# Attention output products in another order: four whole-array products, then eight half-array products

## The chip, the core and the metric

The kernel runs on one core of a Trainium2 chip. Five engines work side by side on one on-chip memory: the matrix engine (TensorE, PE in the profile, its weight loads PEld), VectorE (DVE), ScalarE (ACT), GpSimd (POOL) and SyncE (SP), which here only issues DMA transfers. A matrix product takes a stationary operand that is loaded into the array and streams a moving operand through it; the result goes to PSUM, an accumulator memory in banks. The metric is the device time of one execution in microseconds (us); less is better.

## The reference, cut to what matters

```
# 4 batches, 8 heads, 768 tokens, 48 features per head, all float32
for t in range(S):
    state = alpha[:, :, t, :, None] * state + einsum('bhd,bhe->bhde', k[:, :, t], v[:, :, t])
    y[:, :, t] = einsum('bhd,bhde->bhe', q[:, :, t], state)
x = y.transpose(0, 2, 1, 3).reshape(3072, 384)
h = x @ w_in;  x = (max(h, 0) + m_alpha * min(h, 0)) @ w_out          # expert layer 1, d_ff 2048
h = x @ w_in2; out = where(h >= 1, h, where(h <= -1, 0, (h + 1)**2 / 4)) @ w_out2   # layer 2
```

The first part is a linear attention whose state decays by a factor per feature and step. The two expert layers that follow take nearly all of the arithmetic.

## The kernel before, in words

**Attention in chunks.** The 3072 tokens are cut into 24 chunks of 128, six to a batch. For one chunk, all eight heads together, four functions run in turn. `fetch` brings q, k and alpha to a layout with features on the partitions (tile `T`): up to chunk 9 by transpositions on the matrix engine (`at_in_pe`), from chunk 10 on by a transposition on VectorE (line 205, `X<-nat`) and 16 DMA transfers (line 211, `T<-X`). `at_alpha` builds the running products of the decays on VectorE, `at_qk` scales keys and queries (`K2`, `Q2`). `at_scores` multiplies them for each head (line 247, `sc`), masks the result into `A` (line 252) and, unless the chunk is the last of its batch, transposes `K2` (`kt`, `KT`). `at_out` makes the output `y` of the chunk.

**The output of a chunk.** Two heads form a pair p, so y has four column blocks of 128 tokens, all in one PSUM bank. Each block is the sum of a state product (line 271: the stationary operand is `bd[:, p, :]`, the block-diagonal state of both heads, 128 rows by 128 columns, so it takes the whole array) and two score-value products (line 274: one per head a, with 128 rows by 64 columns of values, so each takes half of the array's columns and writes 64 of the 128 partitions). In the first chunk of a batch there is no state, and the state products are left out. All operands are float32, and each such product runs as two passes on the matrix engine, each with its own weight load: a chunk has 8 passes of state products and 16 of score-value products. Unless the chunk is the last of its batch, eight small products `ds` (line 288) follow, from which VectorE renews `bd` (line 315); GpSimd then divides it by the next chunk's decays (line 332).

**What happens to y.** ScalarE copies y to the high part of `xs`, the input of layer 1 (line 300), VectorE the rest (line 305). The fourth column block holds the last sixteen features of six pairs' heads in a packed form; after the startup it goes by way of `x3` (lines 302 and 307) and six DMA transfers to its places (line 323).

**Startup and the main loop.** The first four chunks run before anything else (`startup`). There the packed block is not moved by DMA: the products of p = 3 come first, ScalarE copies the block to `y3` (line 280), and a further whole-array product per block p = 0 to 2 (line 295, stationary operand `sel`) adds it in. Then the expert layers run in steps: a block of 512 tokens has 16 steps, one per 128 columns of d_ff; in each a product group `hp` (line 429), the activation on VectorE, ScalarE and GpSimd (`g`, `gh`, `gl`; lines 444 to 453), and the second product one step later (line 462 in layer 1, 473 in layer 2). Six blocks are layer 1, six are layer 2. The remaining 20 chunks of attention are laid between the steps of layer 1 by `groups` and `run_slots`; a chunk takes four slots. During the first block the weights of layer 1 are also loaded, joined from 64-bit words (lines 360 to 368) and split. Every engine takes its instructions in the order in which the program is written; there is no scheduler. SyncE's queue carries all DMA issues, in that order too: per chunk 16 of line 211, then the three loads of the next chunk's q, k and alpha (line 157), weight loads (352 to 355), a store (398), the six of line 323 and a load of v (162).

Of the kernel before, what the change touches and what calls it, by code (L numbers as in the profile page):

```python
# [22 lines left out]
def kernel(  # L23
# [13 lines left out]
    nc = tc.nc  # L37
# [5 lines left out]
    NP = H // 2  # L43
    NFC = DFF // P
    ND = DM // P
# [20 lines left out]
    ps_o = main.enter_context(tc.tile_pool(name="ps_o", bufs=1, space=PSUM))  # L66
    ps_a = main.enter_context(tc.tile_pool(name="ps_a", bufs=3, space=PSUM))

# [1 line left out]
    ident = const.tile([P, P], F32, name="ident")  # L70
    mask = const.tile([P, C], F32, name="mask")
    zrev = const.tile([P, NP, SEG], BF16, name="zrev")
# [11 lines left out]
    bd = const.tile([P, NP, P], F32, name="bd")  # L84
# [8 lines left out]
    own = {}  # L93

    def spare_tile(key, shape, name):
        """A tile of the startup in the place of a weight tile that comes later."""
        if key not in own:
            own[key] = wpool.tile(shape, F32, tag=next(spare), name=name)
        return own[key]

    def shared_row(g):
        """Where the last two heads' sixteen features g stand in their own tile."""
        return 16 * g if g < 3 else 64 + 16 * (g - 3)

    sel = spare_tile("sel", [P, ND, P], "sel")

    def setup_consts():
# [31 lines left out]
            if c > 0:  # L139
                nc.gpsimd.memset(v_of(c)[:, :, D:64], 0.0)  # L140

# [1 line left out]
    st = {}  # L143

    NPE = 10
# [16 lines left out]
        eng.dma_start(out=v_of(c)[:, :, 0:D], in_=v[b, :, t0:t0 + C, :].rearrange("h t d -> t h d"))  # L162

    def flag(src, i, col):
        """Sums, into a column, how far the decays lie outside one end of the chunked form's range."""
        junk = p1.tile([P, 768], mybir.dt.uint8, tag="junk", name="junk")
        nc.scalar.activation(junk[:, 0:src.shape[1]], src, AF.Relu, scale=(-1.0, 1.0)[i],
                             bias=bias2[:, i:i + 1], accum_out=acc[:, col:col + 1])
# [6 lines left out]
    NFL = H * S * D // P // 768  # L175

    def load_flags(i):
        """The decays of the first batches, whose chunks pass without their flags."""
        t = p3.tile([P, 768], F32, tag="wst", name="al", padded_shape=[P, 4 * DM])
        nc.sync.dma_start(out=t, in_=alpha[i // NFL].rearrange("h t d -> (h t d)")  # L180
                          .rearrange("(p n) -> p n", p=P)[:, i % NFL * 768:(i % NFL + 1) * 768])
        own["al", i] = t
# [79 lines left out]
    def at_out(c, xdst, startup=False, mid=None):  # L262
        s = st[c]
        vc = v_of(c)
        pool, tag = (ps_h, "h") if startup else (ps_a, "at")
        first, last = c % CPB == 0, c % CPB == CPB - 1
        y = pool.tile([P, NP, C], F32, tag=tag, name="y")

        def emit_y(p, done=True):
            if not first:  # L270
                nc.tensor.matmul(out=y[:, p, :], lhsT=bd[:, p, :], rhs=s["Q2"][:, p, :],  # L271
                                 start=True, stop=False)
            for a in range(2):
                nc.tensor.matmul(out=y[64 * a:64 * a + 64, p, :], lhsT=vc[:, 2 * p + a, :],  # L274
                                 rhs=s["A"][a][:, p, :], start=first, stop=done)

        if startup:
            emit_y(ND)
            y3 = spare_tile(("y3", c % 2), [P, C], "y3")
            nc.scalar.copy(out=y3, in_=y[:, ND])  # L280
        else:
            for p in range(NP):
                emit_y(p)
        if not last:
            ds = pool.tile([P, NP, D], F32, tag=tag, name="ds", padded_shape=[P, NP, P])
            for h in range(H):
                lo = HALVES[h % 2][0]
                nc.tensor.matmul(out=ds[lo:lo + D, h // 2, :], lhsT=s["KT"][:, h // 2, lo:lo + D],
                                 rhs=vc[:, h, 0:D], start=True, stop=True)
        if mid:  # L290
            mid()
        if startup:
            for p in range(ND):
                emit_y(p, False)
                nc.tensor.matmul(out=y[:, p, :], lhsT=sel[:, p, :], rhs=y3, start=False, stop=True)
        xs, o = xdst
        hi, lo = xs[:, 0, :, o:o + C], xs[:, 1, :, o:o + C]
        if not startup:
            x3 = p1.tile([P, 2, C], F32R, tag="x3", name="x3")
        nc.scalar.copy(out=hi, in_=y[:, 0:ND])  # L300
        if not startup:
            nc.scalar.copy(out=x3[:, 0], in_=y[:, ND])

        def low():
            nc.vector.tensor_sub(out=lo, in0=y[:, 0:ND], in1=hi.bitcast(F32))  # L305
            if not startup:
                nc.vector.tensor_sub(out=x3[:, 1], in0=y[:, ND], in1=x3[:, 0].bitcast(F32))

        def state():
            for l, r in HALVES:  # L310
                nv = bd[l:r, :, l:r]
                if first:
                    nc.vector.tensor_copy(out=nv, in_=ds[l:r])
                elif not last:
                    nc.vector.tensor_add(out=nv, in0=ds[l:r], in1=nv)

        for f in (state, low) if startup else (low, state):
            f()
        st.pop(c)
        for g in range(0 if startup else 6):  # L320
            r = shared_row(g)
            d0 = 48 if g % 2 == 0 else 112
            nc.sync.dma_start(out=xs[d0:d0 + 16, :, g // 2, o:o + C].bitcast(F32),
                              in_=x3[r:r + 16].bitcast(F32))

    def at_decay(c):
        """The state before chunk c, divided by the chunk's decays: block diagonal, by pairs."""
        if c % CPB:
            R = st[c]["R"]
            for lo, hi in HALVES:  # L330
                nv = bd[lo:hi, :, lo:hi]
                nc.gpsimd.tensor_mul(out=nv, in0=nv, in1=R[lo:hi, :, 0:1].to_broadcast([D, NP, D]))

# [1 line left out]
    wt = {}  # L335
    stg = {}
    wide = w_in1.dtype != F32
# [18 lines left out]
        stg[layer, fc] = t  # L356

    def words_f32(lo, hi, t, nbias):
        """lo, hi: the words of the float64 t, scaled so that the exponent is rebased."""
        nc.scalar.activation(hi.bitcast(F32), t[:, :, 1].bitcast(F32), AF.Copy, scale=2.0 ** -112)  # L360
        nc.scalar.activation(lo, t[:, :, 0], AF.Relu, scale=2.0 ** -29, bias=nbias)

    def join_f32(f, lo, hi):
        """f: the float of the high word shifted by three, its sign, and the low word's top bits."""
        fu = f.bitcast(U32)
        nc.vector.scalar_tensor_tensor(out=fu, in0=hi, scalar=3, in1=lo,  # L366
                                       op0=ALU.logical_shift_left, op1=ALU.bitwise_or)
        nc.vector.scalar_tensor_tensor(out=fu, in0=hi, scalar=0x80000000, in1=fu,  # L368
                                       op0=ALU.bitwise_and, op1=ALU.bitwise_or)
# [49 lines left out]
    def w_out_of(layer, fc):  # L419
        return [w[:, DM:2 * DM] for w in wt[layer, fc]]  # L420

# [1 line left out]
    def emit_h(layer, fc, xs, n):  # L423
        wh, wl = w_in_of(layer, fc)
        hp = ps_h.tile([P, n], F32, tag="h", name="hp", padded_shape=[P, 512])
# [47 lines left out]
                    nc.tensor.matmul(out=ops[t], lhsT=g[:, t * P:(t + 1) * P], rhs=w,  # L473
                                     start=first, stop=last)

# [1 line left out]
    blk = []  # L477
    t0 = 0
    for n in BLOCKS1:
# [52 lines left out]
    done = [0]  # L532
# [7 lines left out]
    with tc.manual_schedule():  # L540
# [84 lines left out]
            nc.scalar.copy(out=xs[:, 0, d, :], in_=t)  # L625
            nc.vector.tensor_sub(out=xs[:, 1, d, :], in0=t, in1=xs[:, 0, d, :].bitcast(F32))

        # startup: the attention of the first block, chunks overlapped
        load_chunk(0, nc.sync)
        setup_consts()  # L630
        load_chunk(1, nc.sync)
# [67 lines left out]
                if 0 <= i - 4 < 2 * NFB * NFL:  # L699
                    flag(own["al", (i - 4) // 2], i % 2, i - 4)  # L700

# [1 line left out]
    tot = const.tile([P, 1], F32, name="tot")  # L703
    nc.vector.tensor_reduce(out=tot, in_=acc, op=ALU.add, axis=mybir.AxisListType.X)
    fps = ps_a.tile([P, 512], F32, tag="at", name="fps")
# [12 lines left out]


def general_attention(tc, q, k, v, alpha, xT_d):  # L720
    """The recurrence itself, a scan over time for each column of the state: any decay."""
    nc = tc.nc
    B, H, S, D = q.shape
    P = 128
# [1 line left out]
    with ExitStack() as es:  # L726
        cst = es.enter_context(tc.tile_pool(name="g_const", bufs=1))
        one = es.enter_context(tc.tile_pool(name="g_one", bufs=1))
        two = es.enter_context(tc.tile_pool(name="g_two", bufs=2))
# [16 lines left out]
        with tc.For_i(0, B * H, 1) as i:  # L746
            tr = []
            for n, src in enumerate((q, k, alpha, v)):
# [3 lines left out]
                t = one.tile([D, S], F32, tag=f"g_t{n}", name=f"g_t{n}")  # L752
# [6 lines left out]
            y = ps_y.tile([D, 1024], F32, tag="g_y", name="g_y")  # L759
            for e in range(D):  # L760
                vb = ps_v.tile([D, 1024], F32, tag="g_vb", name="g_vb")
                for t, n in spans:
                    nc.tensor.matmul(out=vb[:, t:t + n], lhsT=row[:, e, :], rhs=vT[:, t:t + n],
                                     start=True, stop=True)
                kv = two.tile([D, S], F32, tag="g_kv", name="g_kv")
                nc.vector.tensor_mul(out=kv, in0=vb[:, 0:S], in1=kT)
                state = two.tile([D, S], F32, tag="g_st", name="g_st")
# [4 lines left out]
                for t, n in spans:  # L772
                    nc.tensor.matmul(out=y[:, t:t + n], lhsT=col[:, e, :], rhs=pr[:, t:t + n],
                                     start=(e == 0), stop=(e == D - 1))
# [3 lines left out]


def general_layer(tc, layer, x_src, w_in, w_out, m_alpha, dst, B, to_f32):  # L780
    """One expert layer in float32 products, 128 tokens at a time."""
    nc = tc.nc
    P = 128
    DFF, DM = w_out.shape[0], x_src.shape[0] * P if layer else x_src.shape[1]
    NFC, ND = DFF // P, DM // P
    S = 768
    with ExitStack() as es:
        cst = es.enter_context(tc.tile_pool(name="g_w", bufs=1))
        two = es.enter_context(tc.tile_pool(name="g_l2", bufs=2))
# [11 lines left out]
        for fc in range(NFC):  # L801
            for w, src in ((wi, w_in[:, fc * wn * P:(fc + 1) * wn * P].rearrange("(a p) f -> p a f", p=P)),
# [5 lines left out]
                t = two.tile([P, wn * DM], U32, tag="g_ws", name="g_ws")  # L808
# [3 lines left out]
        with tc.For_i(0, B, 1) as b:  # L812
            for n in range(S // P):
# [9 lines left out]
                for fc in range(NFC):  # L823
                    hp = ps_h.tile([P, P], F32, tag="g_h", name="g_h")
                    for c in range(ND):
                        nc.tensor.matmul(out=hp, lhsT=wi[:, fc, c * P:(c + 1) * P], rhs=xt[:, c, :],
                                         start=(c == 0), stop=(c == ND - 1))
                    g = two.tile([P, P], F32, tag="g_g", name="g_g")
# [53 lines left out]
```

## Time and profile before

| what | value |
|---|---|
| time of three runs, median (lowest to highest) | 974.29 us (974.17 to 976.9) |
| profiled execution, from its first to its last instruction | 972.0 us |
| TensorE busy (PE) | 941.8 us, 97% |
| VectorE, GpSimd, ScalarE busy | 569.1, 374.2, 350.6 us |
| state products, line 271 | 160 passes, 36.4 us |
| score-value products, line 274 | 384 passes, 34.9 + 6.1 us |

The profiled execution has no time of its own besides its span; the median of the runs stands 2.3 us above that span. Passes are pipelined and overlap, so the busy time of a group is not what the engine would save without it. For that the starts of neighbouring passes are compared.

### The profile page before, as it was taken

What the parts mean: (1) busy time and instruction counts of PE and PEld (TensorE: products, weight loads), DVE (VectorE), ACT (ScalarE), POOL (GpSimd) and SP (SyncE); (2) the same over time, 40 slices, a digit from 0 to 9 for tenths busy, and PEclk for the clock granted to TensorE, in tenths of its full rate; (3) what the DMA queues carried; (4) which work ended last, traced back from release to release, by engine and by line L of the source; (5) the groups of instructions that cost most, each with busy time, mean ns of one, the idle gap of its engine ahead of it and who ended that gap; (6) DMA issues with size and microseconds to landing.
All of it is one profiled execution on the core that took longest, in us unless ns stands there. A gap on an engine that the chain in (4) does not pass through costs nothing.

```text
span 972.0 us, 14041 instructions
## 1 busy us (share of the span) xinstructions
PE 941.8 (97%) x5219; PEld 788.0 (81%) x5219; DVE 569.1 (59%) x776; ACT 350.6 (36%) x590; POOL 374.2 (38%) x310
## 2 busy tenths in 40 slices
PE   7898889999999999999999999999999999999996
PEld 6676667777877778778778889999999999999995
DVE  8788887777867777776533433434434334344333
ACT  3544443232332323333223343345533333333332
POOL 3454454344333334433337853323333332233331
PEclk9999999999999999999999999999999999999999
DMA  9976637666766766674123320022000100100001
GB/s 180 189 160 134 137 70 153 144 132 126 154 130 128 151 152 162 133 155 116 39 92 122 107 71 11 1 92 71 24 32 11 55 0 11 55 12 1 33 1 37
DMA packets 227597, 87.15 MB, mean 90 GB/s; under 512 B 194736, under 2 KB 213952, under 8 KB 227520
## 3 DMA queue, kind: packets, MB, share of 16 engines
q1 hardware_dynamic: 227520, 86.16, 38.9%
q8 instruction: 43, 0.70, 0.3%
q14 instruction: 34, 0.28, 0.1%
HBM read 57.42 MB, written 15.73 MB: 75 GB/s over the span
## 4 chain that ended last, share of the span: by engine, by line
PE 82%; DVE 7%; SPq 4%; DMA 4%; issue 2%; ACT 2%; POOL 0%; DVEq 0%; ACTq 0%; POOLq 0%
PE hp L429 37%; PE y L473 20%; PE o L462 17%; PE y L274 2%; PE y L271 2%; PE sc L247 2%; DMA wst<-in_moe_w_in_dram 1%; SPq L157 1%; DVE wf L366 1%; DVE wf L368 1%; DMA wst<-in_moe_w_out_dram 1%; DVE g L444 1%; PE kt L258 1%; SPq L352 1%; DMA xs<-x 1%
## 5 line engine op out<-in xcount | busy, mean ns | idle before, releaser
L453 POOL TENSOR_TENSOR gl<-g,gh 128x512 fp32r<-128x512 f32 x191 | 263.8, 1381 | 505.2 <-ACT gh L452 450.7
L429 PE MATMUL hp<-xs,wh 128*128 128x512 f32 x1152 | 362.0, 396 | 1.3 <-DVE xs L305 0.8
L452 ACT CAST gh<-g 128x512 fp32r<-128x512 f32 (+1 forms) x193 | 119.3, 618 | 425.4 <-DVE g L446 273.7
L429 PEld LDWEIGHTS hp<-xs,wh 128*128 128x128 f32 x1152 | 211.6, 188 | 40.6 <-DVE T L185 0.9
L429 PE MATMUL hp<-xs,wl 128*128 128x512 f32 x576 | 226.7, 394 | 0.0
L449 DVE SCALAR_TENSOR_TENSOR g<-g 128x512 f32<-128x512 f32 (+1 forms) x97 | 68.3, 704 | 214.7 <-ACT g L441 213.2
L429 PEld LDWEIGHTS hp<-xs,wl 128*128 128x128 f32 x576 | 108.4, 188 | 23.1
L441 ACT ACTIVATE g<-hp,half 128x512 f32<-128x512 f32 (+1 forms) x97 | 66.1, 683 | 104.7 <-PE hp L429 101.4
L444 DVE TENSOR_SCALAR g<-hp,malpha 128x512 f32<-128x512 f32 x96 | 71.2, 742 | 55.5 <-PE hp L429 55.3
L462 PE MATMUL o<-gl,wh 128*128 128x512 f32 x288 | 83.5, 399 | 8.0 <-POOL gl L453 7.9
L462 PE MATMUL o<-gh,wh 128*128 128x512 f32 x288 | 83.1, 397 | 7.5 <-ACT gh L452 5.3
L473 PE MATMUL y<-wh,gh 128*128 128x384 f32 x384 | 83.4, 337 | 0.2
L473 PE MATMUL y<-wh,gl 128*128 128x384 f32 x384 | 83.0, 337 | 0.0
L473 PE MATMUL y<-wl,gh 128*128 128x384 f32 x384 | 82.6, 336 | 0.0
L462 PE MATMUL o<-gh,wl 128*128 128x512 f32 x288 | 82.3, 394 | 0.0
L473 PEld LDWEIGHTS y<-wh,gh 128*128 128x128 f32 x384 | 69.5, 188 | 9.1 <-ACT gh L452 1.0
L462 PEld LDWEIGHTS o<-gl,wh 128*128 128x128 f32 x288 | 53.6, 190 | 23.8 <-POOL gl L453 12.9
L462 PEld LDWEIGHTS o<-gh,wh 128*128 128x128 f32 x288 | 53.3, 188 | 23.1 <-ACT gh L452 9.8
L451 DVE TENSOR_TENSOR g<-hp,g 128x512 f32<-128x512 f32 (+1 forms) x97 | 66.5, 686 | 3.4
L446 DVE SCALAR_TENSOR_TENSOR g<-hp,g 128x512 f32<-128x512 f32 x96 | 66.4, 692 | 3.3
L473 PEld LDWEIGHTS y<-wh,gl 128*128 128x128 f32 x384 | 67.9, 188 | 0.4 <-DVE gl L453 0.3
L473 PEld LDWEIGHTS y<-wl,gh 128*128 128x128 f32 x384 | 68.0, 188 | 0.0
(97 smaller groups left out, 930.9 us busy)
## 6 DMA issues: line engine op xcount, KB each, us to landing
wst<-in_moe_w_out_dram SPq DMA_DIRECT2D x32, 384.0 KB, 4.8
T<-X SPq DMA_DIRECT2D x224, 48.0 KB, 2.1
wst<-in_moe_w_in_dram SPq DMA_DIRECT2D x16, 384.0 KB, 5.5
w_d<-wf SPq DMA_DIRECT2D x16, 384.0 KB, 5.6
w<-w_d SPq DMA_DIRECT2D x16, 384.0 KB, 3.0
wst<-in_moe_w_in_dram SPq DMA_DIRECT2D x32, 144.0 KB, 3.4
x_d<-ev SPq DMA_DIRECT2D x18, 256.0 KB, 4.5
x2s<-x_d SPq DMA_DIRECT2D x18, 256.0 KB, 3.0
```

The source lines that it names most:

```text
L247: nc.tensor.matmul(out=scs[h % 2][:, h // 2, :], lhsT=s["K2"][lo:lo + D, h // 2, :], rhs=s["Q2"][lo:lo + D, h // 2, :], start=True, stop=True)
L271: nc.tensor.matmul(out=y[:, p, :], lhsT=bd[:, p, :], rhs=s["Q2"][:, p, :], start=True, stop=False)
L429: nc.tensor.matmul(out=hp, lhsT=w[:, p, :], rhs=xs[:, x, p, :], start=(i == 0), stop=(i == 3 * ND - 1))
L441: nc.scalar.activation(y, x, AF.Relu, bias=half, scale=0.5)
L444: nc.vector.tensor_scalar(out=y, in0=x, scalar1=0.0, scalar2=malpha[:, fc:fc + 1], op0=ALU.min, op1=ALU.mult)
L446: nc.vector.scalar_tensor_tensor(out=y, in0=x, scalar=0.0, in1=y, op0=ALU.max, op1=ALU.add)
L449: nc.vector.scalar_tensor_tensor(out=y, in0=y, scalar=1.0, in1=y, op0=ALU.min, op1=ALU.mult)
L451: nc.vector.tensor_max(out=y, in0=x, in1=y)
L452: nc.scalar.copy(out=hi, in_=y)
L453: (nc.gpsimd if parts == 1 else nc.vector).tensor_sub(out=lo, in0=y, in1=hi.bitcast(F32))
L462: nc.tensor.matmul(out=ops[d], lhsT=w[:, d * P:(d + 1) * P], rhs=g, start=first, stop=last)
L473: nc.tensor.matmul(out=ops[t], lhsT=g[:, t * P:(t + 1) * P], rhs=w, start=first, stop=last)
```

## The change

In `at_out` the twelve products of a chunk are issued by one function, first the four state products of p = 0 to 3, then the eight score-value products. The flag that begins an accumulation (`start`) is set on the first product in the bank alone; before, it was set on the first product of each column block. In the startup all twelve products come ahead of the copy to `y3` and of `ds`, and the three `sel` products follow together. The rest of the difference is comments, which shift the line numbers by up to two: line 271 becomes 274, 274 becomes 278, 288 becomes 290, 295 becomes 296.

```
-        def emit_y(p, done=True):
+        def emit_ys(done):
             if not first:
-                nc.tensor.matmul(out=y[:, p, :], lhsT=bd[:, p, :], rhs=s["Q2"][:, p, :],
-                                 start=True, stop=False)
-            for a in range(2):
-                nc.tensor.matmul(out=y[64 * a:64 * a + 64, p, :], lhsT=vc[:, 2 * p + a, :],
-                                 rhs=s["A"][a][:, p, :], start=first, stop=done)
+                for p in range(NP):
+                    nc.tensor.matmul(out=y[:, p, :], lhsT=bd[:, p, :], rhs=s["Q2"][:, p, :],
+                                     start=p == 0, stop=False, skip_group_check=True)
+            for p in range(NP):
+                for a in range(2):
+                    nc.tensor.matmul(out=y[64 * a:64 * a + 64, p, :], lhsT=vc[:, 2 * p + a, :],
+                                     rhs=s["A"][a][:, p, :], start=first and p == 0, stop=done,
+                                     skip_group_check=True)
+        emit_ys(not startup)
         if startup:
-            emit_y(ND)
             y3 = spare_tile(("y3", c % 2), [P, C], "y3")
             nc.scalar.copy(out=y3, in_=y[:, ND])
-        else:
-            for p in range(NP):
-                emit_y(p)
...
         if startup:
             for p in range(ND):
-                emit_y(p, False)
-                nc.tensor.matmul(out=y[:, p, :], lhsT=sel[:, p, :], rhs=y3, start=False, stop=True)
+                nc.tensor.matmul(out=y[:, p, :], lhsT=sel[:, p, :], rhs=y3, start=False, stop=True,
+                                 skip_group_check=True)
```

On the matrix engine, in the startup (chunk 1), these products stood so before; a name ahead of the arrow is the result, behind it moving and stationary operand, and the sizes are those of the product:

```order
L195 MATMUL tr<-ident,nat_149 128x128 x4
L271 MATMUL y<-Q_268,bd 128x128
L274 MATMUL y<-A,v_139 64x128 x2
L288 MATMUL ds<-v_139,KT 48x48 x8
L271 MATMUL y<-Q_268,bd 128x128
L274 MATMUL y<-A,v_139 64x128 x2
L295 MATMUL y<-y_375,sel 128x128
...
L247 MATMUL sc<-Q_347,K_346 128x128 x8
```

and stand so now:

```order
L195 MATMUL tr<-ident,nat_149 128x128 x4
L274 MATMUL y<-Q_268,bd 128x128 x4
L278 MATMUL y<-A,v_139 64x128 x8
L290 MATMUL ds<-v_139,KT 48x48 x8
L296 MATMUL y<-y_384,sel 128x128 x3
L247 MATMUL sc<-Q_347,K_346 128x128 x8
```

The products of p = 0 to 2 have moved ahead of `ds` and of the copy to `y3`.

On the matrix engine in the main loop (chunk 22, between the second product of a step and the next `hp`), before:

```order
L462 MATMUL o_4099<-gl,wh_950 128x512
L271 MATMUL y<-Q_4376,bd 128x128
L274 MATMUL y<-A,vt 64x128 x2
L271 MATMUL y<-Q_4376,bd 128x128
L274 MATMUL y<-A,vt 64x128 x2
...
L288 MATMUL ds<-vt,KT 48x48 x8
L429 MATMUL hp<-xs,wh_1082 128x512 x2
```

and now:

```order
L464 MATMUL o_4099<-gl,wh_950 128x512
L274 MATMUL y<-Q_4376,bd 128x128 x4
L278 MATMUL y<-A,vt 64x128 x8
L290 MATMUL ds<-vt,KT 48x48 x8
L431 MATMUL hp<-xs,wh_1082 128x512 x2
```

The alternation of line 271 with line 274, four times over, has become one change from one kind to the other. On VectorE, ScalarE, GpSimd and SyncE the order of the instructions is the same as before.

## Rows read from the trace of the kernel before

**Rows 1.** Busy time by stage: stretch, length, busy us (instructions) per engine, clock, DMA, GB/s

```profile
0.00:41.00 41.00, 34.82 (x306) 26.37 (x306) 31.95 (x60) 16.53 (x28) 16.20 (x39) 1.00 1.07 190
41.00:156.00 115.00, 99.13 (x570) 73.71 (x571) 99.73 (x116) 53.79 (x82) 59.48 (x39) 0.99 0.61 128
156.00:490.00 334.00, 333.34 (x2001) 264.36 (x2000) 245.12 (x335) 104.64 (x195) 121.29 (x104) 1.00 0.62 133
490.00:972.00 482.00, 474.55 (x2346) 423.52 (x2345) 192.31 (x267) 175.61 (x286) 177.25 (x129) 1.00 0.13 42
```

**Rows 2.** What the matrix engine waited for, 62 to 156 us: total, times, longest

```profile
PE o L462 <- POOL gl L453: 7.9, 9, 1.3
PE o L462 <- ACT gh L452: 5.3, 8, 1.4
```

**Rows 3.** Timeline of the matrix engine, one chunk (24 passes, then hp): start, length

```profile
485.54 0.38 PE L271 MATMUL y<-Q,bd 128*128 128x128 f32 x2
485.85 0.44 PE L274 MATMUL y<-A,vt 128*64 128x128 f32 x4
486.22 0.49 PE L271 MATMUL y<-Q,bd 128*128 128x128 f32 x2
...
488.58 0.50 PE L429 MATMUL hp<-xs,wh 128*128 128x512 f32 x1
```

**Rows 4.** Timeline of the matrix engine, chunk 6, which has no state product

```profile
111.48 1.09 PE L274 MATMUL y<-A,vt 128*64 128x128 f32 x16
112.40 0.39 PE L288 MATMUL ds<-vt,KT 128*48 128x48 f32 x10
```

**Rows 5.** Timeline of the matrix engine, chunk 1 of the startup

```profile
20.95 1.47 PE L195 MATMUL tr<-ident,nat 128*128 128x128 f32 x12
22.27 0.39 PE L271 MATMUL y<-Q,bd 128*128 128x128 f32 x2
...
26.64 0.38 PE L247 MATMUL sc<-Q,K 48*128 48x128 f32 x2
```

**Rows 6.** State products of line 271 from 156 to 490 us: count, min/median/max ns

```profile
L271 PE MATMUL y<-Q,bd x112: 270/276/378, 164.5 to 488.0; 128*128 128x128 f32 x112
```

**Rows 7.** SyncE's DMA queue, 260 to 285 us: start, length, line, transfer

```profile
259.76 1.38 SPq L323 DMA_DIRECT2D xs<-x  x2
261.86 0.39 SPq L162 DMA_DIRECT2D vt<-in_v_dram  x1
262.63 10.53 SPq L211 DMA_DIRECT2D T<-X  x16
...
278.26 3.79 SPq L323 DMA_DIRECT2D xs<-x  x6
282.29 0.40 SPq L162 DMA_DIRECT2D vt<-in_v_dram  x1
```

**Rows 8.** SyncE's DMA queue, seven chunks later

```profile
405.01 3.82 SPq L323 DMA_DIRECT2D xs<-x  x6
409.13 0.39 SPq L162 DMA_DIRECT2D vt<-in_v_dram  x1
410.01 2.57 SPq L211 DMA_DIRECT2D T<-X  x4
```

**Rows 9.** Timeline of VectorE: the transposition of the inputs of a later chunk

```profile
279.54 1.78 DVE L205 STREAM_TRANSPOSE X<-nat 128x1536 f32<-128x1536 f32 x1 [1.26 <-DMA nat<-in_q_dram]
```

**Rows 10.** Timeline of the matrix engine: first product of the fifth token block

```profile
410.80 0.70 PE L429 MATMUL hp<-xs,wh 128*128 128x512 f32 x2 [0.55 <-DMA xs<-x]
```

**Rows 11.** What VectorE waited for in the startup, 12 to 43 us

```profile
DVE bd L315 <- PE y L271: 2.3, 2, 1.3
DVE xs L305 <- ACT xs L300: 2.2, 4, 0.6
```

**Rows 12.** Stage view of 49 to 53 us, the one stretch with a lower clock

```profile
49.00:53.00 4.00, 4.00 (x14) 3.17 (x13) 3.93 (x5) 0.83 (x1) 0.17 (x1) 0.57 1.28 205
```

**Rows 13.** The wait of the matrix engine ahead of that stretch, 41 to 62 us

```profile
PE o L462 <- ACT T L202: 2.0, 1, 2.0
```


## The prediction

> **What bounds the kernel now.** I read the stages first, then the waits of the matrix engine, then its timeline in one chunk, and last the DMA queue that feeds the attention. The stage view [rows 1] splits the span in four. From 156 to 490 us the matrix engine is busy 333.3 of 334 us, and nearly so from 490 on, where no attention is left. From 41 to 156 us it is busy 99.1 of 115 us, and VectorE, which joins the weight words there, 99.7. The startup up to 41 us shows 34.8 us of the matrix engine beside 32.0 us of VectorE. So time taken from the matrix engine counts in full only behind 156 us. Between 62 and 156 us it waits seventeen times, 13.2 us in sum, for the activations gh and gl, which VectorE begins [rows 2].
>
> **What one chunk costs.** In the timeline of one chunk [rows 3] the reader is to see that a pair, two whole-array passes and four half-array passes, takes (488.58 - 486.22) / 3 = 0.787 us; the first takes 0.68 us. All four take 3.04 us. What are these passes worth without a change of kind? Chunk 6 has sixteen half-array passes in a row [rows 4]: 112.40 - 111.48 = 0.92 us. Twelve whole-array passes of 128 columns in a row, each with its own weights, are the transpositions of the startup [rows 5]: (22.27 - 20.95) / 12 = 0.110 us each. From the first state product to the first score-value product 0.31 us pass for two passes [rows 3], so the change from whole to half takes 0.31 - 0.11 = 0.20 us instead of 0.11. The four half passes before the return take 0.37 us, against 0.23 us for four in chunk 6, so the return costs some 0.1 us more.
>
> Grouped, a chunk is then seven steps of 0.110, one change of 0.20, sixteen half passes in 0.92, and about 0.10 for the return where a whole-array product follows: 0.77 + 0.20 + 0.92 + 0.10 = 2.0 us. That is 1.05 us less than 3.04, or 0.35 us for each of the three pairs of changes that go. Chunks 6, 12 and 18 have no state product and save nothing.
>
> On one point the Trainium skill speaks against it: its page ("TensorE: Matmul & The Clock Gate", The mechanism) says that a weight load runs beside a product in flight only where it goes to other rows of the array. By that, whole-array passes in a row could not hide their loads, and the group would gain little; the third rival below has its price. The twelve passes at 0.110 us do not bear it out.
>
> **Where the gain counts.** From 156 to 490 us line 271 has 112 passes [rows 6], that is 14 chunks of eight: 8 to 11, 13 to 17 and 19 to 23. If the matrix engine stayed the bound, 14 x 1.05 = 14.7 us would go. It does not stay the bound. SyncE's queue issues all transfers in order, and in the middle of this stage it has no time left [rows 7, 8]: sixteen issues of line 211 take 10.5 us, the rest of a chunk's issues about as much. The seven chunks from 262.63 to 410.01 take 147.4 us, 21.1 us each. Between issues there stand steps of some 0.1 us, and longer ones only seven times, the first at 282.1 (0.23 us), the last at 408.8 (0.30 us), 1.8 us in sum. Two consumers already feel it: VectorE's transposition of a later chunk waits 1.26 us for its inputs [rows 9], and the first product of the fifth block waits 0.55 us for the transfers of line 323 [rows 10]. So I take three parts:
>
> - Chunks 8 to 11 come while the queue still has gaps: 4 x 1.05 = 4.2 us.
> - Chunks 13 to 17 and 19 would give 6 x 1.05 = 6.3 us, and the queue lets through what it has to give: 1.8 us, and half of the 1.1 us that stands as gaps just ahead of 262.63 (0.72 and 0.38) [rows 7], in sum 2.4 us. Bounds: 0 if the issues stretch further, 6.3 us if the consumers' slack takes up the rest.
> - Chunks 20 to 23: line 211 runs two chunks ahead, so its last issues, for chunk 23, stand in the slots of chunk 21, and the queue gets free: 4.2 us.
>
> Main loop: 10.8 us.
>
> **The startup.** Chunks 1 to 3 lose three pairs of changes each, 1.05 us, chunk 0 two, 0.70 us: 3.9 us of the matrix engine (the output of chunk 1 takes 26.64 - 22.27 = 4.37 us now [rows 5]). The copy to y3 now waits for all twelve products, but ds stands behind them as cover, as before. What VectorE gets is the end of two waits [rows 11]: 2.3 us in which line 315 may not renew bd before the last state product has read it, which goes, since the state products now come first; and 2.2 us for xs, of which I take a third, as ScalarE has the weights' work in between. That makes 3.0 us (bounds 0, if the transfers, whose share of the DMA engines is full there [rows 1], hold it, and 4.5, if both waits go). From there to 156 us VectorE is busy 99.7 of 115 us and is waited for, so what it begins sooner it ends sooner: the shift should last.
>
> **The first block.** The outputs of chunks 4, 5 and 7 save 1.05 us each on an engine that then waits for gh and gl as it does now [rows 2]: I take 0, with 3.2 us as the other bound.
>
> **Sum.** 972.0 - 10.8 - 3.0 = 958.2 us of span; the median of the runs stands 2.3 us above the span: 960.5 us.
>
> **Rivals.**
> First, the queue does not hold: VectorE's wait [rows 9] is taken up by slack, as it is now. That gives 974.3 - 14.7 - 3.0 = 956.6 us. For it speaks that the matrix engine stands still only some 0.7 us in the whole stage [rows 1, 10]; against it that such a wait recurs, and each chunk would ask for another 1.05 us.
> Second, the queue takes all of the middle and the transfers hold the startup: only 8.4 us remain, 965.9 us. For it speaks that issues stretch: two of line 323 take 1.38 us, 0.69 each, where six take 3.79, 0.63 each [rows 7]. Against it: the gaps that are there can be closed.
> Third, whole-array passes in a row don't hide their loads. The later pairs of a chunk take 0.107 us more than the first [rows 3], whose first load could be done ahead; so a second pass may follow after 0.110 + 0.107 = 0.217 us. Then a chunk takes 7 x 0.217 + 0.20 + 0.92 + 0.10 = 2.74 us and saves 0.30 us; 14 x 0.30 and about 1 in the startup give 969.1 us. The transpositions [rows 5] and the first pair of a chunk speak against it.
> Fourth, slower: the matrix engine waits longer and more often, and its clock falls. In 49 to 53 us the granted clock was 0.57, a stretch at 1.2 GHz [rows 12], after a wait of 2.0 us [rows 13]; at half the clock such a stretch of some 3.4 us (0.43 of 4 us at the lower half, doubled) loses about 1.7 us of work. From the ninth such fall on, 13.8 us are used up, and the kernel is slower: 24 chunks with one fall each would give 974.3 - 13.8 + 41 = 1001 us, twelve of them 981 us. Against it: seventeen waits in the first block brought none.
>
> **How the numbers follow.** The forecast has a chance of 0.55 (its own range 957.5 to 963), the first rival 0.22, the second 0.14, the third 0.05, the fourth 0.02; 0.02 is left for no change at all through something I don't see. The range reaches from the first rival's side to most of the second's: 955.5 to 965. What a measurement of this kernel can tell from no change is about 0.3%, 2.9 us. All but the fourth and the rest lie beyond it: faster 0.96, same 0.02, slower 0.02.
>
> **What would show it.** In the trace of the changed kernel the timeline of one chunk should show the eight state passes in about 0.97 us and the whole in about 2.0 us. The time from 41 to 156 us should be as long as before, and begin some 3 us sooner. From 262 to 410 us the issues of SyncE should follow with no gaps, and the matrix engine should wait some 4 us there, at gh and gl behind a late line 205 and at the first products of the fourth and fifth block. If it waits nowhere there, the first rival is right; if a state pass takes 0.21 us, the third. The forecast is wrong if the stage from 156 to 490 us shrinks by less than 8 or by more than 13 us.

## The result and the profile after

The changed kernel takes 965.96 us (964.43 to 967.44, four runs) where the kernel before takes 975.6 us (974.17 to 978.37): a ratio of 0.9902, 95% interval 0.9879 to 0.9925. In a second set of runs it was 965.82 against 976.06 us, 0.9894 (0.9875 to 0.9914). So it is about 1.0% faster. The forecast was 960.5 us, 955.5 to 965: right in sign and in most of its terms, too good by 5.5 us, and the time lies 1 us above the range.

In the changed kernel line 271 has become line 274, 274 is 278, 288 is 290, 323 is 325, 429 is 431 and 462 is 464; lines 162, 205 and 211 keep their numbers. First one chunk in the timeline of the matrix engine, for [rows 3] (start, length, line, tile and its inputs, count):

```profile
182.08 1.05 PE L274 MATMUL y<-Q,bd 128*128 128x128 f32 x8
183.06 1.09 PE L278 MATMUL y<-A,vt 128*64 128x128 f32 x16
183.99 0.53 PE L290 MATMUL ds<-vt,KT 128*48 128x48 f32 x16
184.44 0.73 PE L431 MATMUL hp<-xs,wh 128*128 128x512 f32 x2
```

The eight state passes and the step behind them take 183.06 - 182.08 = 0.98 us, the sixteen half passes 0.93 us, so the output is done after 1.91 us. The chunk of [rows 3], which has no ds behind it, took 3.04 us up to hp; the same chunk takes 2.01 us now, 1.03 to 1.04 us less. The whole passes start 0.108 to 0.112 us apart. That settles the third rival: passes over the same rows, each with its own weights, do hide their loads, and the sentence of the Trainium skill that it rested on ("TensorE: Matmul & The Clock Gate", The mechanism) does not hold for them here.

Now the stage view with cuts at the same places of the program, for [rows 1] (stretch, length, then busy us of PE, PEld, DVE, ACT, POOL, the granted clock, the DMA engines' share, GB/s):

```profile
0.00:38.00 38.00, 31.77 (x306) 26.44 (x306) 31.88 (x60) 16.58 (x29) 15.45 (x39) 1.00 1.09 191
38.00:153.00 115.00, 95.91 (x570) 71.61 (x571) 99.82 (x116) 53.77 (x82) 60.31 (x40) 1.00 0.64 133
153.00:480.00 327.00, 320.84 (x2003) 261.55 (x2002) 245.10 (x335) 103.57 (x195) 121.06 (x103) 1.00 0.64 136
480.00:965.00 485.00, 477.98 (x2345) 426.08 (x2343) 192.00 (x266) 175.88 (x286) 177.21 (x129) 1.00 0.13 42
```

The startup is 3 us shorter and the first block as long as before. The third stretch is 7 us shorter, where 10.8 us were forecast for the main loop; the matrix engine is now idle there for 6.2 us, where it was for 0.7. The last is 3 us longer, though nothing in it was changed. Four token blocks make up the third stretch, one row each:

```profile
151.00:233.00 82.00, 82.00 (x510) 67.63 (x509) 64.58 (x86) 25.90 (x49) 30.54 (x26) 1.00 0.70 145
233.00:319.00 86.00, 83.10 (x523) 67.22 (x521) 66.19 (x92) 28.50 (x55) 32.57 (x29) 1.00 0.69 144
319.00:404.00 85.00, 82.39 (x500) 66.10 (x500) 63.70 (x87) 27.33 (x53) 30.98 (x26) 1.00 0.70 144
404.00:486.00 82.00, 81.36 (x506) 67.16 (x507) 55.13 (x78) 22.86 (x41) 29.70 (x25) 1.00 0.42 100
```

The reader is to see that the outer two blocks are full of matrix work and the two in the middle are not. From the first product of one block to that of the next it was 86.04, 84.94, 85.24 and 86.13 us; it is 82.27, 85.32, 85.57 and 81.97. What the matrix engine waits for, in the first block (59 to 153 us, for [rows 2]) and in the third stretch (153 to 480 us): total, times, longest:

```profile
PE o L464 <- POOL gl L455: 8.1, 10, 1.3
PE o L464 <- ACT gh L454: 7.3, 9, 1.5
...
PE hp L431 <- DMA xs<-x: 2.9, 3, 1.4
PE o L464 <- ACT gh L454: 2.2, 2, 1.2
PE o L464 <- POOL gl L455: 1.0, 3, 0.4
```

The waits in the middle are those foretold: first products of blocks that wait for the transfers of line 325, and gh behind a late line 205. In the timelines, for [rows 9, 10]:

```profile
319.07 0.71 PE L431 MATMUL hp<-xs,wh 128*128 128x512 f32 x2 [1.43 <-DMA xs<-x]
...
404.64 0.71 PE L431 MATMUL hp<-xs,wh 128*128 128x512 f32 x2 [1.24 <-DMA xs<-x]
...
273.55 1.78 DVE L205 STREAM_TRANSPOSE X<-nat 128x1536 f32<-128x1536 f32 x1 [3.11 <-DMA wst<-in_moe_w_in_dram]
```

And SyncE's queue, for [rows 7, 8]:

```profile
255.56 10.52 SPq L211 DMA_DIRECT2D T<-X  x16
266.18 0.56 SPq L157 DMA_DIRECT2D nat<-in_alpha_dram  x1
...
270.94 4.14 SPq L325 DMA_DIRECT2D xs<-x  x6
275.56 0.39 SPq L162 DMA_DIRECT2D vt<-in_v_dram  x1
...
403.92 1.25 SPq L211 DMA_DIRECT2D T<-X  x2
```

The same seven chunks that took 147.4 us take 403.92 - 255.56 = 148.4 us. At 262.63 us before, now 255.56, the queue was 7.1 us ahead of its old times; at the end of the seven chunks it is 6.1 us ahead. The lead that came in is not kept in full, and nothing is added.

### The profile page after: what moved, and what is told of

It is laid out like the page before. It is cut to its first block, busy times and chain, and to the rows that moved or that the text cites. A ratio compares the mean times of both kernels' runs of the same rounds, so it can differ in the third digit from the quotient of the medians.

```text
span 965.1 us, 14041 instructions
## 1 busy us (share of the span) xinstructions
PE 926.5 (96%) x5219; PEld 785.7 (81%) x5219; DVE 568.8 (59%) x776; ACT 349.8 (36%) x590; POOL 374.0 (39%) x310
## 4 chain that ended last, share of the span: by engine, by line
PE 77%; DVE 7%; DMA 7%; SPq 3%; issue 3%; ACT 2%; POOL 1%; DVEq 0%; ACTq 0%; POOLq 0%
PE hp L431 35%; PE y L475 21%; PE o L464 14%; PE sc L247 2%; DMA xs<-x 2%; PE y L278 2%; DMA wst<-in_moe_w_out_dram 1%; DMA wst<-in_moe_w_in_dram 1%; SPq L211 1%; DVE wf L368 1%; DVE g L446 1%; PE y L274 1%; DVE wf L370 1%; DVE g L448 1%; PE kt L258 1%
```

## The experiments

The theory at the start: from about 233 to 405 us SyncE's issue time sets the pace (Q). Its rivals: the DMA engines' time (B), the latency of a loop through a landing (L), or a cause outside the queue. Ratios are to the kernel before in runs on the same chip.

**The changed kernel again**, five runs, no edit.

> The changed kernel itself, unaltered, as the base for the other runs. Its first trace shows two things that the medians should tell apart: the blocks of layer 2 took 66.99 us each, against 66.35 before, though no instruction of them differs (3.3 us over that layer). If this belongs to the program, the matrix engine's passes of 384 columns should again stand 177 ns apart here, and the span be 965 us; if it varies from one execution to the next, a second trace may show 174 ns and about 962 us.

965.82 us, given above. Block times in its profile are 82.51, 85.96, 85.34 and 82.02 us, so the pattern repeats. But the second layer's blocks take 66.35 us as in the kernel before, where the first profile of the changed kernel had 66.99. The 3 us at the end of that profile belong to the execution, not to the change. The startup varies too: here the first product of the first block stands at 38.92 us, 2.05 us sooner than before and not 3.05, with a granted clock of 0.83 from 20 to 30 us, where both other profiles have 1.00.

**Half of the transfers of line 211 left out**, in both kernels. Half of the tokens of chunks 10 to 23 keep older features, so the output differs.

```
-        for g in range(4):
+        for g in range(2):     # line 211: 8 issues a chunk, not 16
```

> The changed kernel with eight of the sixteen transfers of line 211 left out for chunks 10 to 23 (half of the tokens of these chunks keep an older chunk's features); nothing else. Theory Q (SyncE's queue sets the pace from 234 to 405 us): its load falls by some 5.3 us a chunk, the matrix engine no longer waits at the first products of the blocks nor behind line 205, and each of the blocks from 234 to 320 and 320 to 405 us goes from 85.4 to about 81.7 us; total about 7.5 us faster than the changed kernel, near 958. Rival V (VectorE's and ScalarE's own work sets the pace there): no change beyond 1 us.

> The kernel before with the same eight transfers left out (half of the tokens of chunks 10 to 23 keep an older chunk's features). Theory Q: before the change the queue only just kept up, the matrix engine waited some 0.7 us in that stage, so it gains 0.5 to 1.5 us and no more. The difference of this run and of the changed kernel with the same cut is then the whole gain of the new order, 14.7 us in the main loop and 3.1 us in the startup, 17 to 18 us. If the cut helps the kernel before as much as the changed one, the queue is not what took the gain.

The changed kernel takes 955.63 us (954.48 to 958.51), ratio 0.9783 (0.9763 to 0.9804); the one before 973.46 us, 0.9972 (0.9961 to 0.9984). The four blocks, in the stage view of the changed kernel so cut:

```profile
152.00:234.00 82.00, 82.00 (x511) 67.63 (x510) 64.67 (x86) 26.11 (x49) 30.13 (x27) 1.00 0.56 128
234.00:316.00 82.00, 82.00 (x523) 67.48 (x522) 65.72 (x90) 28.00 (x54) 33.08 (x29) 1.00 0.58 131
316.00:397.00 81.00, 81.00 (x502) 66.49 (x500) 64.54 (x88) 27.56 (x53) 32.25 (x27) 1.00 0.59 132
397.00:479.00 82.00, 82.00 (x510) 67.66 (x509) 54.37 (x78) 23.09 (x41) 30.34 (x26) 1.00 0.34 87
```

All four are full of matrix work. With room in the queue the change is worth 973.46 - 955.63 = 17.8 us, near the 14.7 us forecast for the passes and the 3.1 us of the startup. In the two traces the four blocks give 4.2, 3.1, 3.1 and 4.2 us, 14.6 in sum, and the startup 2.5. Without the change the same cut gives 0.3%. So the passes were sized rightly, and it is the transfers that hold the middle. Issues and bytes fell together here, so Q and B are not told apart. An issue of line 211 takes 0.62 us (median) with all sixteen and with eight alike: a full queue does not make its issues longer.

**The next chunk's loads ahead of the sixteen transfers.** The flags of a chunk come ahead too.

```
 def at_in(c):
     nc.vector.transpose(out=X, ...)
+    at_flag(c)
+    load_chunk(c + 1, nc.sync, (1, 0, 2))
     ...                        # the 16 transfers of line 211
```

> The changed kernel, all its work done, with the loads of the next chunk's q, k and alpha (line 157) issued ahead of the sixteen transfers of line 211 in place of behind them, from chunk 10 on. The queue issues as much as before. Theory L (the pace is set by the round trip: transposition on VectorE, sixteen issues, loads, their landing, next transposition): the loads land 10 us sooner, VectorE's line 205 no longer waits for them, and 5 to 7.5 us go. Theory Q, issue time alone: line 205 no longer waits, but the queue is as full, the waits move to the transfers of line 325 at the first products of the blocks, and 0 to 2.5 us go.

965.43 us, ratio 0.9888 (0.9866 to 0.991): no change against the changed kernel's 0.9894. In its trace, 153 to 420 us, the matrix engine waits:

```profile
PE hp L435 <- DMA xs<-x: 5.0, 2, 3.1
PE o L468 <- POOL gl L459: 0.4, 1, 0.4
PE o L468 <- ACT gh L458: 0.2, 1, 0.2
```

Line 205 no longer waits for its loads. Its waits fall from 11.2 to 5.6 us in this stretch, and those left are mostly for the transfers that still read X (4.3 us). The waits of the matrix engine are as long as before, 5.6 us against 6.1, and now stand at the first products of blocks. Another order in a full queue moves the wait. L asked for a gain of 5 us or more, and falls.

**The six transfers of line 325 on another engine**: once on ScalarE, once on GpSimd. Bytes, order and count stay.

```
-            nc.sync.dma_start(out=xs[d0:d0 + 16, ...
+            nc.scalar.dma_start(...      # first kernel
+            nc.gpsimd.dma_start(...      # second kernel
```

> The changed kernel, all its work done, with the six transfers of line 325 (some 3.9 us of issues a chunk) issued by ScalarE in place of SyncE. The bytes on the DMA engines stay the same. Theory Q (SyncE's issue time is the limit): the queue's 20 us a chunk fall to 16, the waits of the matrix engine from 234 to 405 us (7 to 8 us) go, less what ScalarE's six issues delay gh: 958 to 961 us. Rival B (the DMA engines are the limit, and the queue only shows it): the transfers stay as late, 964 to 967 us. If ScalarE pays more than the queue gave, the time rises and gh is what the matrix engine waits for.

> As the run with ScalarE, but the six transfers of line 325 are issued by GpSimd. Theory Q: the queue is relieved as much, so the waits behind line 205 go; what GpSimd needs to prepare a transfer isn't in any trace so far, and gl waits for it. Between 957 (it costs nothing on the path) and 972 us (each chunk's six cost 0.7 us of the matrix engine's time above what was won).

On ScalarE it takes 1043.09 us (1039.66 to 1044.45), ratio 1.0678 (1.0651 to 1.0705): far from what I expected. What the matrix engine waits for (153 to 420 us), ScalarE's timeline in one chunk, and one stretch of the stage view:

```profile
PE o L464 <- ACT gh L454: 32.8, 9, 5.9
...
275.71 4.03 ACTq L325 DMA_DIRECT2D xs<-x  x6
280.12 0.62 ACT L454 CAST gh<-g 128x512 fp32r<-128x512 f32 x1 [5.28 <-DMA xs<-x]
...
240.00:325.00 85.00, 71.86 (x385) 56.22 (x382) 49.32 (x67) 22.19 (x43) 23.28 (x20) 0.88 0.57 113
```

ScalarE has little to do, but gh is the work that the matrix engine waits for, and here it stands 5.28 us behind six issues. The four blocks grew to 94 to 110 us, 76.5 us in sum, and the waits are not all of it. In them the matrix engine is idle for 49.8 us, 6.2 in the changed kernel, but it is also busy for 361.8 us instead of 328.8 with the same passes, at a granted clock of 0.87 to 0.95 instead of 1.00. So some 44 us are waits, and some 33 us go with the lower clock.

On GpSimd it takes 963.62 us (962.94 to 967.64), ratio 0.9886 (0.9857 to 0.9915), in total no clear difference from the changed kernel's 0.9894. But the middle blocks go from 85.32 and 85.57 to 83.28 and 81.96 us, with the DMA engines' share up to 0.73 and the same bytes. So B falls and Q stands: not the DMA engines but the issues of one queue were the limit. Nor do the transfers land sooner behind their issue: the median of line 325 is 4.8 us on GpSimd, 3.3 on SyncE. The gain is paid back at two places: the first block takes 116.21 instead of 113.56 us, with a granted clock of 0.94 from 40 to 156 us, and GpSimd ends later. Its drain at the end takes 9.87 us, 0.05 in the changed kernel. The group of the issues on GpSimd, count | busy us, mean ns:

```profile
L325 POOL DMA_DIRECT2D xs<-x x120 | 60.7, 512 | 16.8 <-issue 13.1 <-DVE bd L317 2.1 <-DVE x L309 1.6
```

**The second layer's weight loads on ScalarE.**

```
-                load_w(1, i + 1, nc.sync)
+                load_w(1, i + 1, nc.scalar)
```

> The changed kernel, all its work done, with the loads of layer 2's weights (two issues, 1.3 to 2.7 us a chunk) issued by ScalarE in place of SyncE; the bytes stay the same. Theory Q: 1.3 us and more come free in each chunk's 20.4 us, which is about what the queue lacks (85.4 us for four chunks against the 81.8 that the matrix engine asks for, 0.9 us a chunk): 958 to 962 us. Rival B (DMA engines): 964 to 967 us.

984.24 us (980.48 to 988.38), ratio 1.0074 (1.0047 to 1.01): slower than the kernel before, which neither theory said. Its waits, 153 to 420 us:

```profile
PE o L464 <- ACT gh L454: 11.1, 6, 4.7
PE hp L431 <- DMA xs<-x: 3.0, 2, 2.1
```

The two issues themselves take only 0.40 and 0.51 us on ScalarE. The first three blocks grow by some 7 us each. In them (152 to 426 us) the matrix engine is idle for 16.2 us, 5.5 in the changed kernel, and busy for 10.4 us longer, at a granted clock of 0.96 instead of 1.00: about half is waits, half goes with the clock. Why it waits I could not settle: VectorE's line 205 waits 31.3 us from 153 to 420 us, 11.2 in the changed kernel, and line 167 on ScalarE 12.1 us for alpha, 0.9 in the changed kernel, but what delays these loads I did not isolate. So this run does not decide between Q and B.

**The new order in the main loop alone, and in the startup alone.**

```
+        def emit_y(p, done=True): ...  # the old order, pair by pair
-        emit_ys(not startup)
+        ...                            # emit_ys in one of the two, emit_y in the other
```

> The kernel before, with the new order in the main loop alone; the startup keeps the old order. By the traces the startup's part of the gain is 3.1 us and the main loop's 7.2: so 975.8 - 7.2 = 968.6 us. If the startup's 3.1 us were given back later (for the queue is the limit behind 234 us), this run would come out as the changed kernel, 966 us.

> The new order in the startup's four chunks (0 to 3) alone; the main loop keeps the order of the kernel before. If the startup's shift of 3.1 us lasts to the end and the two parts add up: the first block begins at 37.9 us, every later stage is as long as before, 976.1 - 3.1 = 973.0 us. By the medians of the run with the main loop alone (970.5 against 965.8 for both) the startup would be worth 4.6 us: 971.5 us. Rival: the shift is given back where the queue is full, since its issues are no sooner: 975 to 976 us.

Main loop alone: 970.46 us (969.71 to 970.72), ratio 0.9946 (0.9929 to 0.9963). The startup is not shorter (41.92 us to the first product of the first block, 40.97 before), and the blocks take 82.09, 85.95, 86.02 and 83.54 us. Startup alone: 973.75 us (971.67 to 976.81, ten runs), ratio 0.9966 (0.9951 to 0.9981). The two together give 0.54 + 0.34 = 0.88% where the whole change gives 1.0%: they add up within the intervals. But in the profile of the startup alone the first block begins at 38.1 us, 2.9 us sooner, and the second layer at 497.5 us, where it began at 496.9 before: the middle blocks take 87.23 and 86.33 us there, and the matrix engine waits

```profile
PE hp L442 <- DMA xs<-x: 3.1, 2, 1.8
```

So in that execution the whole lead was given back in the full queue, as the rival of that run said. Of its ten times the first five on record are 974.0 to 976.8 us, the profiled one (976.06) among them, and the last five 971.7 to 973.5. How much of the startup's lead lasts in a given execution stays open.

**The half products by halves**: the four of one column half, then the four of the other.

```
-            for p in range(NP):
-                for a in range(2):
+            for a in range(2):
+                for p in range(NP):
                     nc.tensor.matmul(out=y[64 * a:64 * a + 64, p, :], ...
```

> As the changed kernel, but the eight half-array score-value products go by halves: the four of one column half first, then the four of the other. If two half passes run beside each other only where they stand next to each other and use different column halves (in the trace they start 7 ns apart, and a pair takes 0.11 us), eight passes take 0.9 us in place of 0.46, a chunk 0.42 us more: blocks 1 and 4 longer by 1.7 us each, the startup by some 1 us, the middle blocks less: 968 to 971 us. Rival: the array takes two half passes beside each other in whatever order they stand, and nothing changes: 965.9 us.

968.48 us (967.1 to 971.18), ratio 0.9902 (0.9884 to 0.9921): in total no clear difference from the changed kernel's 0.9894, so the trace has to tell. The same chunk in its timeline:

```profile
182.69 1.05 PE L274 MATMUL y<-Q,bd 128*128 128x128 f32 x8
183.67 1.25 PE L278 MATMUL y<-A,vt 128*64 128x128 f32 x13
184.66 0.29 PE L290 MATMUL ds<-vt,KT 128*48 128x48 f32 x2
184.76 0.38 PE L278 MATMUL y<-A,vt 128*64 128x128 f32 x2
184.88 0.29 PE L290 MATMUL ds<-vt,KT 128*48 128x48 f32 x2
184.98 0.27 PE L278 MATMUL y<-A,vt 128*64 128x128 f32 x1
185.09 0.52 PE L290 MATMUL ds<-vt,KT 128*48 128x48 f32 x12
185.54 0.73 PE L431 MATMUL hp<-xs,wh 128*128 128x512 f32 x2
```

The chunk takes 185.54 - 182.69 = 2.85 us up to the next product, 184.44 - 182.08 = 2.36 us in the changed kernel. Passes on the same half start 109 ns apart, where passes on alternating halves start in pairs, 7 ns and then 103 ns apart. But the condition of the expectation, that two half passes run beside each other only where they stand next to each other, is not borne out. It counted eight passes where a chunk has sixteen; one half behind the other, fourteen steps of 109 ns in place of seven would make the chunk some 0.76 us longer, not 0.49, so that the expected 0.42 us came near is luck. By their starts the first four passes stand alone, up to 184.05 us. From 184.16 us on two rows of passes run side by side, each with steps of 109 ns: the second half begins beside the fifth pass of the first. Behind them, passes of line 290 start ahead of the last three of line 278, which come before them in the program. So across the halves the matrix engine does not keep strictly to the order of the program. The outer two of the four blocks (1 and 4, counted from 0) take 83.84 and 83.92 us, 1.57 and 1.95 us more; the middle ones do not get longer by more than 0.7, as they have slack now. The Trainium skill says that different tiles of the array work in parallel ("TensorEngine Tiling (Array Packing)", Key Properties); the trace agrees: where the halves alternate, from the first pair on, and where they do not, from the fifth pass on.

**A version that beats both**: GpSimd issues line 325 for chunks 8 to 19 alone, where SyncE's queue is full.

```
-            nc.sync.dma_start(out=xs[...
+            (nc.gpsimd if 8 <= c < 20 else nc.sync).dma_start(out=xs[...
```

> As the changed kernel, but the six transfers of line 325 are issued by GpSimd for chunks 8 to 19 alone; the first block and the last chunks keep SyncE. Theory Q (SyncE's issue time held chunks 12 to 19): the blocks of these chunks stay at 82 to 83.3 us as with all the issues on GpSimd, the first block is back at 113.6 us, so 2.65 us of that run's price go. If the 3 us at the end belong to any use of GpSimd's queue, they stay: 963.6 - 2.65 = 961 us. If they come from its late issues alone, they go too: 958 us. Rival: what GpSimd's issues gave in the middle came from the first block's longer time (a lead that the queue had built up there): then chunks 12 to 19 are at 85.5 us a block again and the time is 964 to 966 us.

959.66 us (958.62 to 960.61), ratio 0.9815 (0.9799 to 0.983). Against the changed kernel's 0.9894 that is another 0.8%, and the intervals do not touch. The four blocks in the stage view, and what the matrix engine (153 to 420 us) and SyncE's queue (255 to 404 us) still wait for:

```profile
152.00:234.00 82.00, 82.00 (x510) 67.64 (x509) 63.94 (x87) 25.62 (x50) 44.29 (x50) 1.00 0.71 146
234.00:317.00 83.00, 82.55 (x521) 66.91 (x519) 64.90 (x90) 27.86 (x55) 45.70 (x52) 1.00 0.73 149
317.00:399.00 82.00, 81.50 (x499) 66.08 (x500) 63.47 (x87) 27.16 (x53) 44.25 (x50) 1.00 0.73 150
399.00:481.00 82.00, 82.00 (x509) 67.35 (x509) 55.48 (x80) 23.00 (x41) 31.19 (x27) 1.00 0.41 97
...
PE o L465 <- POOL gl L456: 0.6, 2, 0.3
PE hp L432 <- DMA xs<-x: 0.3, 1, 0.3
...
SPq L211 <- DVE X L205: 20.0, 7, 3.6
```

Now the queue waits for VectorE instead of running late. The first block is back at 113.61 us, so the price there came with GpSimd's issues in that block; how much of it was waits and how much the lower clock is not told apart. Of the price at the end part is left: its drain takes 5.95 us, the last block 78.47 us against 77.16.

## Why the prediction was off by 5.5 us, step by step

- **Price of a chunk**: right. 1.05 us forecast, 1.04 measured; with room in the queue all of it counts (the two cut kernels).
- **Startup**: right in this profile. 3.0 us forecast, 40.97 - 37.92 = 3.05 measured at the first product of the first block (2.05 in the second profile); chunk 8's output still stands 3.1 us sooner, so the shift lasts through the first block, which itself gave 0 as forecast. The 2.3 us in which VectorE could not renew bd [rows 11] are gone from its waits. That the shift lasts past the full queue was taken for granted and is not sure (startup alone).
- **Chunks 8 to 11**: 4.2 us forecast, 86.04 - 82.27 = 3.8 measured.
- **Chunks 13 to 17 and 19**: this is the step that failed. "The queue lets through what it has to give: 1.8 us, and half of the 1.1 us that stands as gaps", 2.4 us. It let through nothing: the two blocks got 0.38 + 0.33 = 0.7 us longer (1.1 in the second profile), 3.1 us off, below the bound of 0 that I had set. From the first product of the second block to that of layer 2 the time shrank by 342.3 - 335.1 = 7.2 us, less than the 8 us that I had named as the sign of being wrong. I counted the gaps between issues as time that the queue could give. In the changed kernel they did not close: from 255.56 to 403.92 us eleven gaps above 0.2 us hold 3.9 us beyond 0.1 us each, where by the same count it was 2.2 us (the 1.8 us leaves out a last gap of 0.50 us, just ahead of 410.01). The usual step between issues is 0.045 us (median), not 0.1. The profile lists what the issues of the seven chunks wait for, landings and ScalarE first, then VectorE and the matrix engine, at most 0.7 us each and 8.6 us in sum, 6.3 in the kernel before:

```profile
SPq L211 <- DMA w_d<-wf: 2.1, 5, 0.5
SPq L325 <- ACT gh L454: 1.4, 4, 0.6
SPq L162 <- DMA wst<-in_moe_w_out_dram: 1.4, 4, 0.4
```

So the longer gaps are the queue's own waits, not spare time. That they grew because the work behind them ran late with the queue is the likeliest reading; no run tests it by itself. That the issues "should follow with no gaps" was wrong as a sign; the waits of the matrix engine in the middle, some 4 us forecast, are there (6.1 us in the third stretch).
- **Chunks 20 to 23**: right. 4.2 us forecast, 86.13 - 81.97 = 4.2 measured: the issues of line 211 end there.
- **The sum**: at the start of the second layer the profile is 10.3 us ahead, not 13.8. The span is 6.9 us shorter only, since this execution's second layer took 66.99 instead of 66.35 us a block; in the second profile of the same kernel it did not, and the gain by medians is 10 us. So of the 5.5 us the failed step makes 3.1 and chunks 8 to 11 make 0.4; the rest lies in the spread of executions (the second layer of this one took 3.4 us more; against that, the median stands only 0.8 us above the profiled span now, 2.3 before), that of the kernel before among them, whose profile I started from (974.3 us, with medians of 975.6 to 977.3 later).

The second rival came nearest in the total, 965.9 us, and in part by luck: it gave nothing to the middle, which was right, and nothing to the startup, which was wrong by 3.05 us in this profile and was made up for by the 3.4 us of the second layer. Its ground, that issues stretch, is not seen: those of the seven chunks take 133.4 us in all, 134.2 before; the gaps grew. The first is refuted by the waits in the middle, the third by the passes, the fourth by the clock: 1.00 in each of these stages.

## What to carry to other kernels

A gain per step is to be weighed against the pace of each in-order queue that feeds the step, and small gaps in a full queue are its waits, not its reserve: count them as nothing. When a faster engine meets such a queue, moving issues to another engine over the stretch alone where the queue is full can pay: here GpSimd gave 0.8%. Which engine can take them, its load does not tell. Both have work that the matrix engine waits for (gh 2.2 us, gl 1.0 us in the third stretch), and ScalarE, the less busy one there, cost 77 us, part of it through the lower clock. In this kernel whole-array passes are best kept together, and half-array passes in alternating halves.

## What the runs showed of the hardware

- A change from whole-array to half-array passes and back costs 0.35 us beside the passes themselves; three such pairs of changes fewer gave 1.04 us a chunk.
- Half-array passes on alternating column halves start in pairs, 7 ns apart. Eight in a row on one half start 109 ns apart; the other half's first pass then starts 0.49 us behind the first of them and not behind the eighth, and passes of a later line start before the last of an earlier one.
- The second layer's blocks take 66.35, 66.67 or 66.99 us, by execution, at the same granted clock of 1.0 and without a wait: its passes of 384 columns start 173, 174 or 177 ns apart (medians, 700 to 880 us). That is 3 us in a run, and enough to mislead a comparison of two single profiles.
- An issue of line 325 took 0.59 us on SyncE, 0.60 us on ScalarE and 0.50 us on GpSimd (medians); after GpSimd had issued transfers, its drain at the end of the program took 5.95 us (72 issues) or 9.87 us (120), against 0.05 us.
- Where the six issues had moved to ScalarE and the matrix engine waited for gh, its granted clock was 0.87 to 0.95 in the four blocks, and the same passes kept it busy for 361.8 us instead of 328.8. In the runs with the loads moved ahead and with the main loop alone, the last of the four blocks, behind a wait at its first product, had a granted clock of 0.98 and took 83.55 and 83.54 us, against 81.97 and 82.02 at 1.00.
